# A new opening, a spread of output tiles and deeper load buffers in a fused attention and SwiGLU kernel

## The chip, the cores and the metric

The kernel runs on one core of a Trainium2 chip. The metric is device time of one execution in microseconds (us). Times are medians of several executions; a comparison uses runs of both kernels on the same chip in the same rounds. Spans quoted from a profile are those of one profiled execution and lie some 2 us below the run's time.

PE is the matmul engine (TensorE), PEld its weight load, DVE is VectorE, ACT ScalarE, POOL GpSimd, SP SyncE.

## The reference

Sliding-window attention (window 64, causal) over 8 batches of 576 positions and 8 heads of 64, then a SwiGLU block on the 4608 tokens:

```python
scores = (q @ k.T) / 8;  mask: 0 <= i - j < 64
x   = softmax(scores) @ v            # 4608 x 512 after the heads are joined
g   = x @ w_gate                     # 512 x 1536
out = (g * sigmoid(g) * (x @ w_val)) @ w_out
```

Inputs and output are float32; the kernel computes in bf16.

## The kernel before

The 4608 tokens are cut into 36 chunks of 128 for the attention and into 9 groups of 512 for the block. The parts that matter:

- `F(c, f)`: one column of 128 gate and 128 value features of group c: 8 matmuls, tanh on ACT, two multiplications on DVE.
- `O(c, u)`: one output tile, 12 matmuls with `Wo`, copied by ACT, stored by SP.
- `S(n)`: score matmuls of chunk n; they read `qT` and `kT`, that is q and k transposed. `A(n, n+1)`: the weighted sums of chunk n, with `S(n+1)` in the middle; DVE divides and writes `xb(n)`.
- `xb(n)` must be transposed into `xT`, the input of F: by PE and ACT (`X`) or by a DMA transpose (`XD`).
- q and k must be transposed too: by PE (`T`) for the first chunks, by DMA transposes (`TD`) for the later ones.
- `load(n)`: q, k, v of chunk n by GpSimd's DMA queue, which also carries the weights. `warm(n)`: n dummy matmuls on zeros.

```python
    def TD(self, n):                      # cut: names of buffers
        g.op("sp", dma_start_transpose(kT(n), kn), ...)
        g.op("sp", dma_start_transpose(qT(n), qn), ...)

    def XD(self, n):
        g.op("sp", dma_start_transpose(xT(n), xb(n)), reads=[xb halves], ...)

    def A(self, n, nxt=None):
        ...
        first = g.op("pe", phase(0), ...)
        masks = self.S(nxt, None, True) if nxt is not None else []
        g.op("pe", phase(1), ..., after=[first])
        ...                               # DVE: reciprocal, multiply -> xb(n)

    # main loop (cut)
        for c in range(1, NFC):
            for u in range(4):
                n = 4 * c + u + 4 + (c > 1)
                load(n + 4)
                self.F(c, 3 * u)
                self.A(n, n + 1 ...)
                if n >= self.ND:
                    self.XD(n)
                if self.ND <= n + 3 < NCH:
                    self.TD(n + 3)        # three chunks ahead
                self.F(c, 3 * u + 1)
                if c > 1 and not late:
                    self.O(c - 1, u)
                ...
                self.F(c, 3 * u + 2)
```

In the traces each engine takes up its blocks of instructions in the order of the program (SP's three transposes below start at 116.59, 117.83 and 119.13 us, XD first). XD and TD share SP, so in each block TD waits behind XD, and XD waits for `xb(n)`.

The softmax here doesn't subtract the row's maximum and nothing guards it: scores larger than these inputs give would overflow.

## Time and profile before

| | before |
|---|---|
| time, median | 343.28 us at first, 344.26 us with one run more |
| span of the profiled run | 343.4 us |
| PE busy | 329.1 us, 96% |
| first real column F(0,0) starts | 16.38 us |
| PE without a gap from | 99.5 us on |

Parts 1 and 2 of the page: busy time, and the span in 40 slices, in tenths (PEclk is the granted PE clock).

```profile
PE 329.1 (96%) x3459; PEld 161.2 (47%) x3459; DVE 213.7 (62%) x457; ACT 141.4 (41%) x248; POOL 109.2 (32%) x145
...
PE   7779969999999999999999999999999999999996
...
PEclk9999998999999999999999999999999999999999
```

The page is of a run of 345.12 us, slower than the median. In the later jobs this kernel's runs lie in steps: those near 343.4 us have a mean granted clock of 1.00, those near 345.2 us 0.995, those near 346.8 us 0.99.

PE is the limit nearly everywhere. Only the first six slices leave room, and in the seventh the clock dips. That dip is seen in the PE timeline (start, duration, engine, line, operation, output<-inputs, shape, count; in brackets idle time just before and what ended it).

```profile
51.38 4.36 PE L537 MATMUL ps<-Wo,hT 128*128 128x512 bf16 x12 [1.91 <-DVE hT L523]
...
57.41 2.76 PE L537 MATMUL ps<-Wo,hT 128*128 128x512 bf16 x12
...
114.33 0.43 PE L399 MATMUL ps<-qT,kT 64*64 64x128 bf16 x24
...
122.85 0.42 PE L399 MATMUL ps<-qT,kT 64*64 64x128 bf16 x24
```

PE waited 1.91 us for DVE before the first output tile, which then took 4.36 instead of 2.76 us. The last two lines are the scores of two neighbouring chunks in steady state: 8.52 us from one to the next, with no wait. What SP does between them (same columns):

```profile
116.59 1.20 SPq L495 DMA_TRANSPOSE xT<-xb  x1
117.83 1.26 SPq L368 DMA_TRANSPOSE kT<-kn  x1
119.13 1.27 SPq L371 DMA_TRANSPOSE qT<-qn  x1
```

The transposes are issued one after another, 1.3 us each. This last one landed 6.2 us after its issue, at 125.3 us. That is later than the next scores at 122.85 us, but these do not need it: it is for the chunk after.

### The profile page before, as it was taken

To read this page: it belongs to the slowest core of one execution; us is meant where nothing else is said; L and a number is where in the kernel's file an instruction comes from. 1 tells how busy PE (TensorE), PEld (TensorE's weight loads), DVE (VectorE), ACT (ScalarE), POOL (GpSimd) and SP (SyncE) were. 2 spreads that over 40 slices of the span, in tenths; PEclk is the share of its full clock that TensorE was granted. 3 is DMA by queue.
4 is the path that set the end of the run, shared out by engine and by line. 5 is a ranking of instruction groups with operands and counts; after the bars stand their busy time and mean duration, and the time that the engine had idled before them with its cause. 6 is when DMAs were issued, how large, how long until landed. Compare 5 with 4: busy or idle time off the path is not lost.

```text
span 343.4 us, 8182 instructions
## 1 busy us (share of the span) xinstructions
PE 329.1 (96%) x3459; PEld 161.2 (47%) x3459; DVE 213.7 (62%) x457; ACT 141.4 (41%) x248; POOL 109.2 (32%) x145
## 2 busy tenths in 40 slices
PE   7779969999999999999999999999999999999996
PEld 3456434554444444444444444444444444444444
DVE  3567772378976666666666666666666666555520
ACT  2753633665544444444444444444444442333321
POOL 7999541465605334333333343333000000000000
PEclk9999998999999999999999999999999999999999
DMA  8999999999969999999999999999833211000012
GB/s 203 187 196 173 174 184 148 115 123 107 154 76 138 122 125 130 129 123 123 122 128 128 126 122 126 129 121 124 121 63 92 73 51 48 33 31 31 32 52 102
DMA packets 161844, 39.33 MB, mean 115 GB/s; under 512 B 146320, under 2 KB 157328, under 8 KB 161808
## 3 DMA queue, kind: packets, MB, share of 16 engines
q0 software_dynamic: 113152, 17.83, 73.4%
q1 hardware_dynamic: 46432, 19.80, 28.7%
q10 hardware_dynamic: 2224, 1.18, 1.3%
q8 instruction: 27, 0.44, 0.5%
q14 instruction: 9, 0.07, 0.1%
HBM read 37.75 MB, written 9.44 MB: 137 GB/s over the span
## 4 chain that ended last, share of the span: by engine, by line
PE 78%; DVE 11%; ACT 3%; DMA 3%; POOL 2%; issue 2%; POOLq 0%
PE ps L513 45%; PE ps L537 27%; DVE uu L521 3%; DVE hT L523 3%; PE ps L448 3%; DMA Wv<-in_moe_w_val_dram 3%; PE ps L399 2%; DVE xb L466 2%; DVE pt L414 1%; ACT sig L519 1%; ACT qT L360 1%; POOL va L330 1%; PE ps L566 1%; POOL Wg L336 1%; DVE kT L359 1%
## 5 line engine op out<-in xcount | busy, mean ns | idle before, releaser
L521 DVE SCALAR_TENSOR_TENSOR uu<-sig,ps 128x512 bf16<-128x512 bf16 (+1 forms) x112 | 74.6, 666 | 88.8 <-ACT sig L519 88.8
L513 PE MATMUL ps<-xT,Wg 128*128 128x512 bf16 (+1 forms) x448 | 111.9, 372 | 0.9 <-ACT xT L489 0.9
L513 PE MATMUL ps<-xT,Wv 128*128 128x512 bf16 (+1 forms) x448 | 111.6, 371 | 0.3 <-DMA Wv<-in_moe_w_val_dram 0.3
L537 PE MATMUL ps<-Wo,hT 128*128 128x512 bf16 x420 | 97.7, 384 | 1.9 <-DVE hT L523 1.9
L519 ACT ACTIVATE sig<-ps 128x512 bf16<-128x512 f32 (+1 forms) x112 | 65.1, 582 | 57.1 <-PE ps L513 56.5
L523 DVE SCALAR_TENSOR_TENSOR hT<-uu,ps 128x512 bf16<-128x512 bf16 (+1 forms) x112 | 74.8, 667 | 3.9
L264 POOL DMA_DIRECT2D qn<-in_q_dram x36 | 30.6, 852 | 127.6 <-DMA qT<-qn 99.7
L513 PEld LDWEIGHTS ps<-xT,Wv 128*128 128x128 bf16 x448 | 43.7, 98 | 50.0 <-issue 0.5
L537 PEld LDWEIGHTS ps<-Wo,hT 128*128 128x128 bf16 x420 | 41.1, 99 | 51.8 <-issue 2.1
L513 PEld LDWEIGHTS ps<-xT,Wg 128*128 128x128 bf16 x448 | 40.5, 98 | 43.1 <-ACT xT L489 1.6
L549 ACT ACTIVATE ost<-ps 128x512 f32<-128x512 f32 x35 | 20.9, 597 | 93.0 <-PE ps L537 93.0
L409 ACT ACTIVATE pt<-ps 128x512 bf16<-128x512 f32 x72 | 38.9, 595 | 22.2 <-PE ps L399 21.9
L330 POOL DMA_DIRECT2D va<-in_v_dram x40 | 34.9, 878 | 0.8 <-DVE ident L227 0.8
L466 DVE TENSOR_TENSOR xb<-ps,rc 128x256 bf16<-128x256 f32 x72 | 30.6, 424 | 2.5
L264 POOL DMA_DIRECT2D kn<-in_k_dram x36 | 30.8, 860 | 0.0
L414 DVE TENSOR_TENSOR pt<-pt,mask 128x512 bf16<-128x512 bf16 x64 | 24.0, 416 | 0.0
L448 PE MATMUL ps<-va,pt 64*64 64x65 bf16 x1088 | 22.7, 196 | 0.9 <-DVE pt L414 0.6
L448 PEld LDWEIGHTS ps<-va,pt 64*64 64x64 bf16 x1088 | 15.2, 106 | 15.1 <-issue 10.6
L463 DVE RECIPROCAL rc<-ps 128x4 f32<-128x4 f32 x72 | 12.5, 173 | 10.1 <-PE ps L448 10.1
L399 PE MATMUL ps<-qT,kT 64*64 64x64 bf16 (+1 forms) x864 | 15.5, 201 | 2.4 <-ACT xT L489 1.8
L399 PEld LDWEIGHTS ps<-qT,kT 64*64 64x64 bf16 x864 | 12.4, 108 | 4.2 <-ACT xT L489 2.0
L360 ACT ACTIVATE qT<-ps 128x512 bf16<-128x512 bf16 x8 | 4.8, 597 | 13.3 <-DVE kT L359 13.2
(44 smaller groups left out, 78.2 us busy)
## 6 DMA issues: line engine op xcount, KB each, us to landing
out_dram<-ost SPq DMA_DIRECT2D x35, 256.0 KB, 3.3
va<-in_v_dram POOLq DMA_DIRECT2D x32, 128.0 KB, 6.5
qn<-in_q_dram POOLq DMA_DIRECT2D x28, 128.0 KB, 4.3
kn<-in_k_dram POOLq DMA_DIRECT2D x28, 128.0 KB, 6.1
Wo<-in_moe_w_out_dram POOLq DMA_DIRECT2D x2, 768.0 KB, 15.2
Wg<-in_moe_w_gate_dram POOLq DMA_DIRECT2D x5, 256.0 KB, 10.7
Wv<-in_moe_w_val_dram POOLq DMA_DIRECT2D x5, 256.0 KB, 12.0
fk<-in_k_dram SPq DMA_DIRECT2D x2, 512.0 KB, 7.3
```

The source lines that it names most:

```text
L264: self.g.op("pool", lambda e, d=d, a=a: e.dma_start(d, a), writes=ks, dma=True)
L330: g.op("pool", lambda e, d=d, a=a: e.dma_start(d, a), writes=ks, dma=True)
L399: r = e.matmul(sv[h][o:o + 64, c, q0:q1], self.kT[ps, c, kk:kk + 64], qT[ps, c, q0:q1], start=not biased, stop=not biased or c == 3 and kk ...
L409: g.op("act", lambda e, po=po, si=si: e.activation(po, si, ACTF.Exp, scale=SCALE), reads=[bk], writes=[pk])
L414: "dve", lambda e: e.tensor_tensor(po, po, m, ALU.mult), reads=[pk, "mask"], writes=[pk]))
L448: r = e.matmul(av[half][ws, j, :], pt[ks, h, ws], vv[ks, h, 0:65], start=key == q[0], stop=key == q[-1])
L466: g.op("dve", lambda e, xo=xo, rb=rb, a=av[half]: e.tensor_tensor(xo, a[:, :, 0:64], rb, ALU.mult), reads=[bk, ("rc", ir)], writes=[("xb", ...
L513: r = e.matmul(bank[:, 0:n], W[:, kk, f * 128:f * 128 + 128], xT[:, kk, t0:t1], start=(kk == 0), stop=(kk == NK - 1))
L519: g.op("act", lambda e: e.activation(sig[:, 0:n], G[:, 0:n], ACTF.Tanh, scale=0.5), reads=[gk], writes=[("sig", i)])
L521: g.op("dve", lambda e: e.scalar_tensor_tensor(uu[:, 0:n], sig[:, 0:n], 1.0, G[:, 0:n], ALU.add, ALU.mult), reads=[("sig", i), gk], writes ...
L523: g.op("dve", lambda e: e.scalar_tensor_tensor(hT[:, f, t0:t1], uu[:, 0:n], 0.5, V[:, 0:n], ALU.mult, ALU.mult), reads=[("uu", i), vk], wr ...
L537: r = e.matmul(OB[:, :], hT[:, f, 128 * u:128 * u + 128], self.Wo[:, f, :], start=(f == 0), stop=(f == NF - 1))
```

## The change

The intent: let everything in the opening arrive in the order of need (only chunks 0 and 1 by the float32 loads on SP's and ACT's queues, chunks 2 and 3 by GpSimd's queue), fill PE's gaps with dummy matmuls, load Wo after chunk 8, and spread the output tiles of group 0 over the columns of group 1, where DVE was short of time. To let loads run ahead, the q and k buffers go from 4 to 6, v from 8 to 10; DMA transposes start with chunk 8 in place of 12.

```diff
-    NQ = 4
-    NV = 8
+    NQ = 6
+    NV = 10
-    ND = 12
+    ND = 8
... opening, cut: first_loads and first_cast for chunks 0 and 1 only
         W(0, 1)
+        self.load_qk(2)
         W(1, 2)
+        self.load_qk(3)
         self.load_v(2)
         self.load_v(3)
-        for f in range(2, 12, 2):
+        W(2, 4)
+        ...
+        for f in range(4, 12, 2):
             W(f, f + 2)
+        for n in range(4, 8):
+            load(n)
...
         self.S(0, b0)
         self.S(1, b1)
+        self.warm(4)
         self.A(0)
+        self.warm(2)
         self.A(1)
... more of warm(); T(2), T(3) on PE; load(8); Wo; load(9); group 0
-        self.O(0, 0, None, "f")      # and O(0,1..3) in a row, with X and T between
+        self.S(8)
+        self.O(0, 0)
+        def block(n):                # cut: returns at once for n >= NCH
+            load(n + 4)
+            self.A(n, n + 1 if n + 1 < NCH else None)
+            if n != 11:
+                self.XD(n)
+            if n + 2 < NCH:
+                self.TD(n + 2)       # two chunks ahead
+        place = {(1, 1, 0): 8, (1, 1, 2): 9, (1, 2, 1): 10, (1, 3, 0): 11,
+                 (2, 0, 0): 12, (2, 1, 0): 13, (2, 1, 2): 14, (2, 2, 1): 15, (2, 3, 0): 16}
...
-                if self.ND <= n + 3 < NCH:
-                    self.TD(n + 3)   # three chunks ahead
... then one block per three columns, with O(c - 1, u) after the second
```

TD(n+3) became TD(n+2). With ND = 8, chunks 8 and 9 too are now transposed by DMA: TD(8) and TD(9) stand in the opening, after A(6, 7) and A(7).

## The prediction

> **What bounds it now.** TensorE: busy 329.1 of 343.4 us (page, part 1). From 99.5 us on, the chain of waits is all TensorE: one unit (three gate/value columns, one output tile, attention of one chunk) takes 8.52 us without a gap. Only the front can be shortened. Issue times there (a full column 1.73 us, an output tile 2.59, attention of a chunk 0.75, T 0.45, X 0.22) against the PE timeline: first real column at 16.4 us; about 2.5 us lost up to 29 us; 4-5 up to 51 us, where VectorE is on the chain (2 x 0.69 us per column, 1.85 us of attention per chunk); 1.9 us waiting for hT before the first output tile, which then runs 4.36 instead of 2.76 us (windows: granted clock 0.83); about 2 us in group 1, which has VectorE work but no output tiles. Some 11-12 us in all.
>
> **What the change gains.** Group 0's outputs go between group 1's columns, which removes the 1.9 + 1.6 us and most of the VectorE-bound loss. Casting q in halves should put the first column near 14.5 us. But columns 2 and up wait for weights: GpSimd needs 0.7-1.1 us per issue and the DMAs move some 190 GB/s, so column 2 stays near 20 us, and chunk 4's q and k, just in time before (32 us), land no sooner. Wo, issued near 40 us instead of 32, should land near 51-52, before its first use near 58. Dummy matmuls fill idle time. Three X and two T fewer on PE: 1.5 us. Net gain estimated: 5-9 us.
>
> **What it costs.** The DMA transposes of q and k used to be issued three chunks ahead; now two. S(n+2) runs inside A(n+1), and its transposes are queued on SyncE behind XD(n), which waits for xb(n). From the trace: S start to xb done 1.8 us, XD 1.3, kT 1.3, then qT from issue to landing 2.5-6.2 us, median 4.8 (2.5 only once the loads have ended). The Trainium skill ("DMA: Bandwidth & Descriptors", Anatomy of one DMA) says that waits sit in the issuing sequencer; the SP timeline agrees: kT and qT go 1.3 and 2.6 us after XD. So S to S needs 4.4 + L, about 9 us (L near 4.5). PE work between S's: 8.5 us in steady state, but 6.8, 6.8 and 4.2 in groups 1 and 2, where chunks lie closer. Estimated PE idle: about 19 us in groups 1 and 2 (four times 2.2, twice 4.8, small rest), 0-8 us up to about chunk 27, then none. Idle stretches may lower the clock again ("TensorE: Matmul & The Clock Gate", Part 1, has idleness halve it; this trace shows 0.83 granted after 1.9 us): 0-3 us.
>
> All of this is on the critical path: TensorE executes in order.
>
> **Predicted time:** 343.3 - 7 + 19 = 355 us; 80% range 343 to 368. Faster by over 2%: 0.07; within 2%: 0.26; slower: 0.67.
>
> **What would show it.** PE waiting at the score matmuls for the DMA writing qT: twice 4-5 us, about ten times 1-3 us between 65 and 140 us; PE busy below 93%; first output tile near 58-60 us, unstalled; first column at 14-15 us, T(4) still near 32 us; XD to qT landing 7 us.
>
> **What would make it wrong.** Transposes landing in 2.5-3 us because loads run further ahead (six q/k buffers): then the stalls cost some 7 us and the time is unchanged. Wo or chunk 9 landing late: several us more. A lookahead chain that does not bind: near 336 us.

## The result

The changed kernel took 371.79 us (371.06 to 373.02, 4 runs) against 344.26 us (342.99 to 346.81, 4 runs) for the kernel before. The ratio is 1.079, 95% interval 1.072 to 1.087. The direction was as predicted; the time lay above the range.

The page, parts 1 and 2, of the changed kernel:

```profile
PE 328.5 (89%) x3428; PEld 166.3 (45%) x3467; DVE 213.3 (58%) x459; ACT 138.9 (38%) x249; POOL 112.7 (30%) x151
...
PE   7986998856699766999999998999899999999997
...
PEclk9999999899699998999999999999999999999999
```

PE's recorded busy time is as before (328.5 us) and the span is 26.3 us longer (369.7 against 343.4). Not all of that is idle time: 4.5 us that the page counts as idle are missing records (line 508 below), so PE was idle some 22 us longer and busy some 4 us longer. The waits of PE, longest in total first (us in total, times, longest):

```profile
PE ps L394 <- DMA qT<-qn: 23.1, 11, 4.3
PE ps L508 <- issue: 4.5, 27, 0.3
PE ps L350 <- DMA kn<-in_k_dram: 2.8, 1, 2.8
```

Line 394 is the score matmul, line 350 the PE transpose of chunk 4. The 27 small pieces on line 508 are no idle time: there the count of Wg matmuls is 3 in place of 4, so one record is missing, mostly 0.16 us. Two neighbouring waits in group 1, on PE and then on SP:

```profile
86.78 0.41 PE L394 MATMUL ps<-qT,kT 64*64 64x128 bf16 x21 [1.64 <-DMA qT<-qn]
...
90.84 0.32 PE L443 MATMUL ps<-va,pt 64*64 64x65 bf16 x16
95.50 0.64 PE L394 MATMUL ps<-qT,kT 64*64 64x128 bf16 x24 [4.34 <-DMA qT<-qn]
...
96.70 1.49 PE L508 MATMUL ps<-xT,Wg 128*128 128x512 bf16 x3 [0.33 <-DVE rc L458]
97.98 1.91 PE L508 MATMUL ps<-xT,Wv 128*128 128x512 bf16 x4
```

```profile
88.64 1.20 SPq L490 DMA_TRANSPOSE xT<-xb  x1
89.89 1.26 SPq L363 DMA_TRANSPOSE kT<-kn  x1
91.19 1.26 SPq L366 DMA_TRANSPOSE qT<-qn  x1
```

This is the loop that sets the pace. The scores of chunk 11 run at 86.78 us; xb(10) is done and XD issued at 88.64; qT(12) is issued at 91.19 and lands 4.3 us later, at 95.5; only then can the scores of chunk 12 run. From S to S it takes 8.7 us, though PE has only 4.4 us of work between them (8.72 less the wait of 4.34). The next columns then run slowly: a Wv group takes 1.91 us instead of 1.03.

Where the 26.3 us come from, by the traces:

| part | us | from |
|---|---|---|
| waits of the scores for qT, groups 1 and 2 | +19.6 | 2.13 + 3.67 + 1.64 + 4.34 + 1.73 + 1.74 + 4.34 |
| matmuls at a lower clock after three of them | about +5 | stretches from S to the next output tile against the same stretches elsewhere |
| longer period afterwards | +6.3 | 26.3 minus the lag of 20.05 us at O(2,0) (133.61 to 153.66 us) |
| the opening and the rest | about -4.6 | what is left of that lag: 20.05 - 19.6 - 5 |

The lag is how much later the changed kernel starts the same output tile, O(2,0). The last row is a remainder: it makes the table add up and carries the errors of the other rows.

One wait of the first row is not the lookahead's. The 2.13 us at chunk 9 are for TD(9), which stands in the opening and is the same in e1. Its qT landed at 65.8 us here, and between 64.8 and 66.5 us in e1, e2 and e4 to e8, whether chunk 8's scores came at 57 or at 63 us; only e9, which loads chunk 9 before Wo, has it at 61.0. With this wait and the 1.6 us of slow clock after it counted to the opening, the opening gained about 1 us and not 4.6, which fits e1 below.

### The profile page after: what moved, and what is told of

Same layout as the page of the kernel before. It is cut to its first block, busy times and chain, and to the rows that moved or that the text cites. A ratio compares the mean times of both kernels' runs of the same rounds, so it can differ in the third digit from the quotient of the medians.

```text
span 369.7 us, 8222 instructions
## 1 busy us (share of the span) xinstructions
PE 328.5 (89%) x3428; PEld 166.3 (45%) x3467; DVE 213.3 (58%) x459; ACT 138.9 (38%) x249; POOL 112.7 (30%) x151
## 4 chain that ended last, share of the span: by engine, by line
PE 33%; issue 31%; POOL 19%; DMA 14%; SPq 1%; DVE 1%; ACT 0%; POOLq 0%
PE ps L508 19%; PE ps L532 12%; DMA qT<-qn 6%; POOL qn L263 6%; POOL va L325 5%; DMA va<-in_v_dram 5%; POOL kn L263 3%; DMA kn<-in_k_dram 3%; POOL Wg L331 1%; POOL Wv L331 1%; PE ps L443 1%; PE ps L394 1%; SPq L363 1%; PE ps L561 1%; SPq L490 1%
## 5 line engine op out<-in xcount | busy, mean ns | idle before, releaser
L508 PE MATMUL ps<-xT,Wv 128*128 128x512 bf16 (+1 forms) x467 | 114.1, 367 | 0.1
L508 PE MATMUL ps<-xT,Wg 128*128 128x512 bf16 (+1 forms) x435 | 107.4, 367 | 5.8 <-issue 4.5
L532 PE MATMUL ps<-Wo,hT 128*128 128x512 bf16 x417 | 95.8, 380 | 0.3 <-issue 0.2
L263 POOL DMA_DIRECT2D qn<-in_q_dram x38 | 34.5, 922 | 134.1 <-DMA qT<-qn 133.9
L508 PEld LDWEIGHTS ps<-xT,Wv 128*128 128x128 bf16 x468 | 46.3, 99 | 49.4 <-issue 3.2
L508 PEld LDWEIGHTS ps<-xT,Wg 128*128 128x128 bf16 x468 | 42.8, 99 | 42.3 <-issue 1.6
L394 PE MATMUL ps<-qT,kT 64*64 64x64 bf16 (+1 forms) x864 | 16.4, 207 | 24.2 <-DMA qT<-qn 23.1
L325 POOL DMA_DIRECT2D va<-in_v_dram x40 | 36.5, 920 | 1.6 <-DVE ident L226 0.8
L263 POOL DMA_DIRECT2D kn<-in_k_dram x38 | 34.6, 915 | 2.8 <-DMA Wo<-in_moe_w_out_dram 2.8
L443 PEld LDWEIGHTS ps<-va,pt 64*64 64x64 bf16 x1088 | 16.9, 109 | 15.6 <-issue 12.1
L311 PE MATMUL ps<-wz 128*128 128x512 bf16 x25 | 8.0, 458 | 1.4 <-DVE wz L225 1.3
```

Of the source, the lines that this page charges most:

```text
L263: self.g.op("pool", lambda e, d=d, a=a: e.dma_start(d, a), writes=ks, dma=True)
L325: g.op("pool", lambda e, d=d, a=a: e.dma_start(d, a), writes=ks, dma=True)
L394: r = e.matmul(sv[h][o:o + 64, c, q0:q1], self.kT[ps, c, kk:kk + 64], qT[ps, c, q0:q1], start=not biased, stop=not biased or c == 3 and kk ...
L443: r = e.matmul(av[half][ws, j, :], pt[ks, h, ws], vv[ks, h, 0:65], start=key == q[0], stop=key == q[-1])
L508: r = e.matmul(bank[:, 0:n], W[:, kk, f * 128:f * 128 + 128], xT[:, kk, t0:t1], start=(kk == 0), stop=(kk == NK - 1))
L532: r = e.matmul(OB[:, :], hT[:, f, 128 * u:128 * u + 128], self.Wo[:, f, :], start=(f == 0), stop=(f == NF - 1))
```

## The experiments

The theory: two chunks of lookahead are too few, because TD(n+2) is queued behind XD(n), which hangs on xb(n), and all of it sits between two score blocks. Rivals: (1) the DMA engines are busier and the transposes land too late; (2) the new opening or the new placement loses by itself.

### e1: three chunks ahead again

```diff
+        self.TD(10)                  # between S(8) and O(0, 0)
-            if n + 2 < NCH:
-                self.TD(n + 2)
+            if n + 3 < NCH:
+                self.TD(n + 3)
```

> The changed kernel with the DMA transposes of q and k issued three chunks ahead again, all else as changed. Lookahead theory (S to S is bound by xb, XD, kT, qT and its landing, 8.65 us in the trace, wherever PE work between is shorter): the waits of the score matmuls for qT go from 23 us to under 2 us, the granted clock stays 1.00 after 60 us, time 337 to 341 us (front gain of 5 to 6 us is left). Rival 1, the transposes land too late because the DMA engines are busier (six q/k buffers let loads run ahead): waits of 10 us or more stay, time above 355. Rival 2, the opening and the spreading of outputs lose by themselves: time above 348 with few qT waits.

Measured: 343.27 us (341.95 to 344.98), ratio to before 0.997 (0.993 to 1.002). The waits of PE:

```profile
PE ps L350 <- DMA kn<-in_k_dram: 4.2, 1, 4.2
...
PE ps L394 <- DMA qT<-qn: 0.3, 1, 0.3
```

The wait for qT fell from 23.1 to 0.3 us and the time by 28.5 us (medians of two jobs). Rival 1 falls on its own number. Between 60 and 100 us the transposes of q landed later than in the changed kernel. The DMA view of that stretch (engine, kind, count, median us from issue to landing), first the changed kernel, then e1:

```profile
qT<-qn SPq DMA_TRANSPOSE x4, 4.2
```

```profile
qT<-qn SPq DMA_TRANSPOSE x7, 7.7
```

7.7 us (median) with three chunks of lookahead left 0.3 us of waits; 4.2 us with two (but 7.5 at chunk 10) left 19.6. What was not as expected: only 0 to 1 us was left of the opening's gain, not 5 to 6. The wait for chunk 4's k is the reason to look at next: the five profiled runs with this opening (the changed kernel, e1, e2, e4, e7) waited 2.8 to 4.2 us there.

### e2: the transposes ahead of XD in the queue

```diff
-            if n != 11:
-                self.XD(n)
             if n + 2 < NCH:
                 self.TD(n + 2)
+            if n != 11:
+                self.XD(n)
```

> The changed kernel, still two chunks ahead, but in each block the transposes of q and k are queued on SyncE before XD, which waits for xb. If the queue order behind XD is what makes two chunks too few: the 1.7 us waits and the later ones go; only the two tight places (chunks 10 to 11 and 15 to 16, 4.2 us apart) keep about 2 us each, as the transposes there sit behind an output store; time 340 to 345 us. If two chunks are too few whatever the order, or the landing is at fault: 355 or more.

Measured: 350.82 us (349.49 to 351.53), ratio to before 1.018 (1.014 to 1.022). Waits for qT: 5.1 us in three places (2.7 at chunk 10, 0.9 at 12, 1.4 at 16):

```profile
PE ps L394 <- DMA qT<-qn: 5.1, 3, 2.7
```

Queue order alone, still two chunks ahead, recovers 21 of the 28.5 us: from chunk 17 on no wait is left. The number expected (340 to 345 us) was too low. The transposes of chunk 10 were issued behind the store of the first output tile and landed 7.9 us after issue, so the largest wait came at chunk 10, where I expected none. Order and distance are not two parts that add up: distance alone (e1) takes away all 28.5 us, order alone 21.

### e3: two chunks ahead in the kernel before

```diff
-                if self.ND <= n + 3 < NCH:
-                    self.TD(n + 3)
+                if self.ND <= n + 2 < NCH:
+                    self.TD(n + 2)
...
-                    self.TD(n + 4)           # after the extra chunk 12
+                    self.TD(n + 3)
```

> The kernel before with one thing changed: transposes two chunks ahead in place of three. Lookahead theory: one wait of about 5 us where chunks 12 and 13 lie 3.1 us apart (near 97 us), then the period of a unit grows from 8.52 to about 8.8 us up to chunk 27: time 351 to 358 us. If the loss comes from the opening or the new placement only: 343 to 347 us.

Measured: 358.29 us (356.75 to 361.41), ratio 1.039 (1.033 to 1.045), just above what was expected. One wait of 4.0 us came at the scores of chunk 14, inside A(13), where blocks 12 and 13 lie close:

```profile
103.27 0.65 PE L399 MATMUL ps<-qT,kT 64*64 64x128 bf16 x24 [4.04 <-DMA qT<-qn]
```

The period grew in places to 8.8 us and, four times, to about 10. So the shorter lookahead alone costs 4%, some 14.7 us, without any other part of the change. That it costs 28.5 us in the changed kernel fits the denser placement of chunks there.

### e4: three chunks ahead only from chunk 17 on

```diff
-            if n + 2 < NCH:
-                self.TD(n + 2)
+            for m in ([n + 2] if n < 16 else [18, 19] if n == 16 else [n + 3]):
+                if m < NCH:
+                    self.TD(m)
```

> The changed kernel with three chunks ahead only from chunk 17 on; groups 1 and 2 as changed. Gives the share of the late part: the period from chunk 18 on goes back to 8.52 us and the time falls by 5 to 7 us to 365 to 367 us, with some 19 to 20 us of qT waits left in groups 1 and 2. If the late waits are hidden elsewhere: no change from 371.8.

Measured: 364.42 us (363.5 to 366.67), ratio 1.059 (1.054 to 1.064), 7.4 us less than the changed kernel and just below the range expected. The waits left for qT are 16.2 us, fewer than the 19 to 20 expected. The late part thus holds about 7 us of the loss and groups 1 and 2 the other 21 (28.5 - 7.4). From chunk 18 on the period is 8.52 us again.

### e5: loads of chunks 4 to 7 between the weights

This builds on e1, to find where the gain of the opening went.

```diff
         for f in range(4, 12, 2):
             W(f, f + 2)
-        for n in range(4, 8):
-            load(n)
+            load(2 + f // 2)
```

> The changed kernel with three chunks ahead (as e1) and, in the opening, the loads of chunks 4 to 7 issued one by one between the weight pairs from column 4 on, in place of after all weights. Theory: what is left of the opening's gain is eaten by the PE transposes of chunk 4, which wait 4.2 us for k and then run 1.4 us at a lower clock. Expected: that wait under 0.5 us, no new wait for weights over 1 us, time 336 to 339 us (some 5 us below e1's 343.3). Rival, the DMAs as a whole are too slow and another load waits instead: 341 to 344 us.

Measured: 342.98 us (342.67 to 343.75), ratio 0.996 (0.991 to 1.000). The rival was right. The wait for chunk 4's k is gone and the scores of chunk 8 come 5.5 us earlier (57.28 instead of 62.80 us), but the time is given back at the next scores:

```profile
65.34 0.41 PE L394 MATMUL ps<-qT,kT 64*64 64x128 bf16 x21 [4.67 <-DMA qT<-qn]
```

That is chunk 9. Its k landed 16.6 us after its issue, at 57 us, behind Wo in the same queue, and its transpose another 8 us later.

### e6: without the twelve new dummy matmuls

This builds on e5; the five `warm(...)` calls between the first scores and the first real column are taken out.

> e5 without the twelve dummy matmuls between the first scores and the first real column (the thirteen and two ahead of them stay, as before). If they hold the clock: real columns from 15 us on run at a lower granted clock and the time rises by 1 to 3 us over e5. If the gaps there are too short for the clock to fall: within 0.5 us of e5.

Measured: 344.87 us (343.98 to 345.2), 1.9 us above e5; the intervals of the two ratios overlap, but the slowest run of e5 (343.75) is below the fastest of e6 (343.98). The windows view decides (window, length, busy time of PE, PEld, DVE, ACT, POOL, granted clock, DMA share, GB/s), first e5, then e6:

```profile
12.00:14.00 2.00, 1.76 (x45) 1.06 (x42) 1.81 (x7) 0.46 (x2) 2.00 (x4) 1.00 1.94 160
14.00:16.00 2.00, 1.63 (x12) 0.69 (x11) 0.43 (x2) 1.00 (x2) 1.87 (x4) 1.00 2.25 143
16.00:18.00 2.00, 2.00 (x27) 1.85 (x25) 1.26 (x3) 0.77 (x2) 1.81 (x9) 1.00 1.69 156
```

```profile
10.00:12.00 2.00, 0.80 (x40) 0.46 (x28) 0.16 (x1) 2.00 (x4) 2.00 (x4) 1.00 1.86 139
12.00:14.00 2.00, 1.36 (x36) 0.85 (x36) 1.86 (x8) 0.29 (x2) 2.00 (x3) 0.62 1.95 156
14.00:16.00 2.00, 1.11 (x7) 0.73 (x8) 0.14 (x1) 0.92 (x2) 1.81 (x5) 0.50 2.35 145
16.00:18.00 2.00, 2.00 (x11) 1.42 (x10) 0.84 (x2) 0.38 (x1) 1.87 (x9) 0.50 1.62 171
```

Without the dummies the granted clock is 0.50 from 14 to 18 us, and column 2 starts at 22.0 instead of 20.65 us. The dummies do their work in this opening, and are worth 1.4 us there in the profiles.

### e7: dummy matmuls inside the long waits

The changed kernel, two chunks ahead, with `warm(k)` before S(n+1) in A(n) for n = 8, 9, 10, 15 (k = 8, 13, 14, 14).

> The changed kernel as it is (two chunks ahead), with 8, 13, 14 and 14 dummy matmuls put before the score matmuls that wait longest (in chunks 8, 9, 10, 15), that is some 10 us more work for PE inside the waits. Clock theory: the columns after these waits no longer run slow (they took 2.5 to 3.0 us in place of 1.73), so the time falls by 2 to 5 us, to 367 to 370 us, though PE does more. If the slow clock is not caused by the idle waits: no fall, 371 to 376 us.

Measured: 367.29 us (365.09 to 369.15), ratio to before 1.066 (1.059 to 1.073), so 4.5 us less than the changed kernel by the medians of two jobs; the two intervals just overlap. I placed two of the four fillings one block too early: the 4.3 us waits belong to the scores of chunks 12 and 17, and those stayed unfilled. That makes a control inside one run. Chunk 9, filled, then chunk 12, unfilled:

```profile
65.51 1.90 PE L311 MATMUL ps<-wz 128*128 128x512 bf16 x8
67.34 0.41 PE L394 MATMUL ps<-qT,kT 64*64 64x128 bf16 x22
...
68.72 1.03 PE L510 MATMUL ps<-xT,Wv 128*128 128x512 bf16 x4
...
97.65 0.41 PE L394 MATMUL ps<-qT,kT 64*64 64x128 bf16 x22 [4.17 <-DMA qT<-qn]
...
99.52 1.91 PE L510 MATMUL ps<-xT,Wv 128*128 128x512 bf16 x4
```

After the filled wait a Wv group takes 1.03 us, after the unfilled one 1.91. In the changed kernel, with neither filled, the groups at these two places took 1.60 and 1.91 us: only the filled place changed. PE's busy time rose by 10.7 us and the kernel did not get slower. So the idle waits cost twice: themselves, and the clock after them.

### e8: group 0's output tiles in one piece, on e5

```diff
-        self.O(0, 0)
+        for u in range(4):
+            self.O(0, u)
...
                     if s == 1 and not late:
-                        self.O(c - 1, u)
+                        if c > 1:
+                            self.O(c - 1, u)
```

> e5 with the four output tiles of group 0 in one piece before the rest of group 1, as in the kernel before, so that group 1's columns have none among them. If spreading them is what takes VectorE off the path: VectorE waits of 2 to 5 us come back in group 1, and the time is 2 to 5 us above e5. If it is worth nothing: within 1 us of e5. Some qT waits may appear, as chunks then lie closer together.

Measured: 344.41 us (343.82 to 345.21), 1.4 us above e5, with overlapping intervals. This was inconclusive: e5 lost 4.7 us at chunk 9; with the tiles in a row chunk 9 comes later anyway and does not wait for its transposes, but chunk 11 now waits for its own, 4.9 us. One wait hides the other.

### e9: chunk 9 loaded before Wo, on e5

```diff
+        load(9)
         self.load_wo(0, 6)
         self.load_wo(6, 12)
-        load(9)
```

> e5 with the loads of chunk 9 issued before Wo in place of after it. Theory: in e5 the score matmuls of chunk 9 waited 4.7 us because its k and q landed 16.6 us after issue, behind Wo, at 57 us. Expected: that wait under 0.5 us, at most 1 us of waiting for Wo, granted clock 1.00 around 65 us, time 335.5 to 338.5 us, faster than the kernel before by about 2 percent. Rival, the DMAs are full until about 57 us whatever the order, so Wo or chunk 10 waits instead: 340 to 343 us.

Measured: 339.66 us (339.54 to 340.39, 6 runs), ratio 0.985 (0.980 to 0.990). This beats both kernels, by 1.5% over the kernel before (the interval excludes no change, though the gain is under the 2% that this study counts as faster) and by 8.6% over the changed one (339.66 / 371.79). It is 1.2 us above the range expected. Chunk 9 no longer waits, the granted clock stays 1.00, but part of the rival holds too: Wo landed only at 58.6 us, the transposes of chunk 8 took 12 us to land, and chunks 8 and 10 wait a little:

```profile
58.56 0.45 PE L394 MATMUL ps<-qT,kT 64*64 64x128 bf16 x24 [1.42 <-DMA qT<-qn]
...
70.54 0.41 PE L394 MATMUL ps<-qT,kT 64*64 64x128 bf16 x21 [1.19 <-DMA qT<-qn]
```

### e10: e9 with the output tiles in one piece

The edit is that of e8.

> e9 with the four output tiles of group 0 in one piece, as in the kernel before, now without the wait that e5 and e8 shared. If spreading them over group 1 takes VectorE off the path: 2 to 4 us above e9. If it is worth little, as e8 against e5 hinted (1.4 us): under 1.5 us above e9.

Measured: 345.2 us (344.32 to 346.11, 6 runs), ratio 1.001 (0.996 to 1.005): 5.5 us above e9, more than expected, and not for the reason expected. No DVE wait of any size came back. Instead:

```profile
83.52 0.64 PE L394 MATMUL ps<-qT,kT 64*64 64x128 bf16 x24 [4.83 <-DMA qT<-qn]
```

Without the tiles between them, the scores of chunks 9 and 10 lie 4.2 us apart (70.11 and 74.31 us), those of chunk 11 would follow 4.4 us later, and then even three chunks of lookahead are too few. In this kernel, spreading the output tiles pays because it spaces the chunks.

## Why the prediction was right or wrong

The prediction was right in direction and in the mechanism of the waits, and too low in size: 355 us, at most 368, against 371.8. What failed is the sum: two costs that it named but counted as nothing, and a gain in the opening that was hardly there.

- **Right:** "S to S needs 4.4 + L, about 9 us (L near 4.5)". The trace has 8.7 us, with L from 4.0 to 4.3 us at most of the waits. The Trainium skill says that a semaphore wait sits in the issuing sequencer and not in the DMA engine ("DMA: Bandwidth & Descriptors", Anatomy of one DMA). SP's timeline agrees, with kT and qT 1.25 and 2.55 us after XD, and e2 shows it by experiment: moving TD ahead of XD in the queue removes 21 us.
- **Right:** "Estimated PE idle: about 19 us in groups 1 and 2 (four times 2.2, twice 4.8, small rest)". Measured 19.6 us, in seven waits of 1.6 to 4.3 us. The places are right: chunks 10, 11, 15 and 16 (8.8 us together, as predicted) and twice 4.34 at chunks 12 and 17. That the sums agree so closely is in part luck: the four were 3.67, 1.64, 1.73 and 1.74, the first after a landing of 7.5 us, and the 2.13 us at chunk 9 were not in the estimate of the lookahead.
- **The step that failed:** the sum "343.3 - 7 + 19". It counted two of the terms named just before it at the bottom of their ranges, that is as nothing: "0-8 us up to about chunk 27" was 6.3 us by the trace (7.4 us by e4), and the clock, "0-3 us", was about 5 us by the trace. A range whose low end is 0 belongs in a sum with its middle. But the middles (4 and 1.5) would have given only 360.8 us; the rest is the low clock, beyond its range, and the opening.
- **Also mis-sized:** "Net gain estimated: 5-9 us", used as 7, was about 4.6 us by the table, and about 1 us once chunk 9 is counted to the opening; e1 has 0.3. Of the loss it meant to win back, the 1.6 us of the slow first output tile were in the profile but not in the faster runs. The prediction named this under "What would make it wrong" ("Wo or chunk 9 landing late: several us more") and left it out of the sum. Chunk 4's k was named as landing "no sooner", near 32 us. It landed at 33.9 us, PE was ready at 31.1, and so PE waited 2.85 us there (4.2 us in e1). I had not put PE's own earlier arrival against that time. The four misses together (6.3 + 5 + 2.4 + 0.6 = 14.3 us) are the distance from the 355.3 us of the sum to 369.6 us, the 343.3 us of before with the 26.3 us added. They must be, since the table's last row is a remainder. The other 2.2 us to 371.8 come mostly from the start of the sum: 343.3 us is the median of the first runs, while the profiled run of 345.12 us is the one that the 26.3 us are measured from.
- **Half right:** "First column at 14-15 us" was 15.74 us; "first output tile near 58-60 us, unstalled" was 61.0 us and unstalled; "PE busy below 93%" was 89%; "about ten times 1-3 us between 65 and 140 us" were four, and one of 3.67.
- **On the clock:** The Trainium skill says that idleness of about 3.4 us halves it ("TensorE: Matmul & The Clock Gate", Part 1) and that the window is free-running. The 2.13 us wait at chunk 9 lowered the clock (granted 0.76 between 64 and 68 us), the 3.67 us wait at chunk 10 did not (1.00), and 4.34 us did. The windows view of the changed kernel suggests why the length of a wait alone does not decide. The clock is 0.50 from 66.07 to 69.48, from 93.38 to 100.20 and from 141.16 to 144.58 us, that is for 3.41 or 6.83 us, and these starts lie 8 and 14 times 3.41 us apart: a fixed grid, which agrees with a free-running window. In the stretch of 3.41 us just before each start PE was busy for 1.28, 1.19 and 0.00 us. The grid cut the wait at chunk 10 in two, and both stretches that hold it have more work, 1.60 and 1.39 us. So a stretch need not be wholly idle to count: 1.28 us of work in 3.41 was little enough here. (The 0.83 in the prediction is the mean over 10 us around such a stretch: in the kernel before the clock is 0.50 from 51.2 to 54.6 us.)
- **Where the intended gain went:** it existed, and each time a later load took it back. In the changed kernel chunk 9's transposes took most of it, and the lookahead buried the rest; with that undone (e1) PE waited for chunk 4's k; with that moved (e5), for chunk 9's transposes; with that moved too (e9), 3.9 us remain by the medians of the same rounds.

Open: why the transposes land in 2.4 us in one place and in 8 or 12 in others. The Trainium skill says that each DMA engine takes turns between its queues packet by packet ("DMA: Bandwidth & Descriptors", Queues, rings and completion order). The long landings all fall where GpSimd's loads are under way, and the short ones (2.4 to 2.5 us) where these pause or have ended, which fits, but no run here varied the loads alone. Nor did a run take back the deeper q, k and v buffers alone: e1 has them and waits 0.3 us for qT, so they are not the loss, but whether they lengthen the landings is open.

## What to carry to other kernels

When work is moved closer together, recompute every prefetch distance in time, not in steps: the distance that hid a chain at 8.5 us per step no longer hides it at 4.2. Look at what stands ahead of a transfer in its issuing queue; a DMA whose data are long ready is still late behind one that waits. And when summing a prediction, put the middle of each uncertain cost into the sum, and weigh the named risks there too.

## What the Trainium skill lacked or had wrong

- "DMA: Bandwidth & Descriptors" gives a bandwidth for DMA transposes but no time to landing; the time for a DMA transpose in "VectorE: DVE Perf Modes" (The three transpose paths) is for a single block of 128x128. Here a transpose of 128x512 bf16 inside SBUF took 2.4 to 2.5 us where the loads had paused or ended, mostly 4 to 6 us beside loads, 7.7 us (median) in the stretch of e1 shown above, and 12 us in e9 with Wo in the queue.
- "TensorE: Matmul & The Clock Gate" speaks of idle windows of about 3.4 us. How busy a window may be and still count as idle is not said. In the changed kernel windows with PE busy for 0, 35 and 37% of 3.41 us were followed by half the clock, windows with 41 and 47% were not. The busy share in such a window is not the whole rule: in e4 one of 41% (122.16 to 125.58 us) was followed by half the clock, and in e6 no single gap between 10 and 16 us was longer than 0.93 us and PE was busy for 40 to 68% of each 2 us, and yet the granted clock fell to 0.50.
